# A third routing round inside the branch, and the second round's placement on GpSimd

## The chip, the cores and the metric

The program runs on one core of one Trainium2 chip. The metric is the device time of one execution in microseconds (us). Five engines work side by side, each through a queue of its own and in order: TensorE (PE, the matmuls), VectorE (DVE), ScalarE (ACT), GpSimd (POOL) and SyncE (SP, which issues most DMAs). An instruction that waits holds up all that stand behind it on its engine.

## What is computed

Attention with random features over 2304 tokens of 512 values feeds a gated feed-forward layer, and that feeds a mixture of 8 experts, of which each token takes one:

```
logits = x @ w_gate + modality_bias[modality_id]          # (2304, 8)
e_idx  = argmax(logits, axis=1)
gate_w = softmax(logits)[token, e_idx]
for e in range(8):
    mask = e_idx == e
    h = maximum(x[mask] @ w1[e], 0)                       # 512 -> 1024
    out[mask] = gate_w[mask, None] * (h @ w2[e])          # 1024 -> 512
```

How many tokens an expert gets is known only at run time.

## The kernel before, in words

Tokens lie in 18 tiles of 128, worked through the feed-forward layer in 6 groups of 3 tiles (`moe1_group`). All products are three matmuls of split operands (`mm3`, lines 166 to 168): a high and a low half of each factor, where `split` (lines 171 and 172) makes the halves, ACT the high one and DVE the rest.

The expert layer works in **slots**. A slot is 2 or 3 token tiles of one expert: its weights come by 8 DMAs on SP's queue, are split in 16 steps (one ACT cast, one DVE subtraction each), its token rows are gathered by an indirect DMA on POOL (line 1131), turned by PE (line 1143) and split; then come 8 steps of first-layer matmuls (`h`), the relu with its rest `ul` on DVE (line 1185) and second-layer matmuls (`acc`, lines 166 to 168), and the result rows are scaled (lines 1204 and 1206) and scattered by POOL (line 1208). `slot_prefetch` brings one slot's weights and rows while `slot_body` of the slot before runs.

Which expert and which tokens a slot gets is found by **routing**, in rounds. The first round covers the 15 tiles of groups 0 to 4 and fills 6 slots, four of 2 tiles and two of 3; what it cannot place, and the last 3 tiles, go to the second round (18 tiles as candidates), which fills one slot of 3 and one of 2. For what is still left the second round also maps up to 16 further slots of 2 tiles, which run in nested `If`s behind the static ones (`more`). So the second round's map has 1 x 3 + 1 x 2 + 16 x 2 = 37 columns, rounded to 38, of which the first 5 are static.

`finish_route` is a list of steps on DVE: `count` (full tiles per expert), `place` (prefix sums over experts, how much each slot kind takes), `experts` (the expert of each slot, read by SP for the weight DMAs), `offsets`, `ranks`, `ranks2` (each token's destination), `columns`, `columns2`, and then one pair of steps for every 3 tiles: on DVE three products `f_mv` (line 960) and three one-hot tiles `f_lh` (line 964), on PE three matmuls into `inv` (line 969). Step `d` reads `inv` and gives the gather indices, the scatter indices and the gate weights. `f_lh` has 3 buffers (line 963), one for each tile of a pair; `f_mv` takes one of the 3 buffers of the tag `row`, which result rows use too.

The order on every engine is the order in which the program issues the instructions, and it is written out with **due times**: `T.at(due, step)` puts a step in a heap, and `T.step(dt)`, called ahead of each piece of matmul work, first issues all steps that are due and then advances the clock by that piece's planned length (0.66 or 0.98 for half of a first-layer step of 2 or 3 tiles, 0.65 for a tile of the second layer). Constants at the top of the file place the steps: `LQ` the logit loads and dot products of the last group (first number their distance), `FO` and `FC` the distances of the routing steps and of the pair halves, `PF` and `PG` the weights and the gather of the first slot, counted from the first round's start. A slot's matmuls take 8 x (2 x 0.66 + 2 x 0.65) = 20.96 of this plan time with 2 tiles and 31.28 with 3. The order of the slots is 2, 2, 2, 2, 3, 3 (first round), then 3, 2 (second).

The logits of a group are 24 DVE instructions (line 737) on weight rows brought by 8 DMAs on SP's queue (line 732); `group_route` turns them into the one-hot `OH` and, with two matmuls, the ranks `RK`. For the last group all this runs beside the first slots.

Of the kernel before, what the change touches and what calls it, by code (L numbers as in the profile page):

```python
# [23 lines left out]
PF = 4.33  # L24
PG = -0.42
PD = 1.5
LQ = (8.5, 4.52, 0.96)
LATE = 6
FO = 1.9
FC = 0.6  # L30
# [88 lines left out]
def kernel(  # L119
# [60 lines left out]
    with tc.manual_schedule():  # L180
# [544 lines left out]
        def logits_rows(g, xrows, lp, ld, lt):  # L725
# [66 lines left out]
        def finish_route(r):  # L792

            A, B2 = rounds
            second = r is B2
            C, nt = r.C, r.nt
            ts = slice(0, nt)
            nsl = r.n2 + r.n3 + r.cap
# [3 lines left out]
            FAR = -1e5  # L802

# [3 lines left out]
            def sums(x, k):  # L807

                s0 = t_(f"f_s0{k}", [P, k, 2 * E])
                s1 = t_(f"f_s1{k}", [P, k, 2 * E])  # L810
                nc.vector.memset(s0[:, :, 0:E], 0.0)
                nc.vector.memset(s1[:, :, 0:E], 0.0)
                nc.vector.tensor_copy(s0[:, :, E:], x)
                for a, b, n in ((s0, s1, 1), (s1, s0, 2), (s0, s1, 4)):
                    nc.vector.tensor_tensor(out=b[:, :, E:], in0=a[:, :, E:], in1=a[:, :, E - n:2 * E - n], op=ALU.add)
                return s1[:, :, E:]

            def count():
# [15 lines left out]
                nc.vector.tensor_tensor(out=ab[:, 1, :], in0=ab[:, 1, :], in1=h, op=ALU.min)  # L834
                nc.vector.tensor_tensor(out=ab[:, 0, :], in0=h, in1=ab[:, 1, :], op=ALU.subtract)

            def place():

                ab = st["ab"]
                st["inc"] = inc = sums(ab, 2)  # L840
                st["pre"] = pre = t_("f_pre", [P, 2, E])
                st["got"] = got = t_("f_got", [P, 2, E])
                nc.vector.tensor_tensor(out=pre, in0=inc, in1=ab, op=ALU.subtract)
                for i, n in enumerate((r.n2, r.n3)):
                    nc.vector.tensor_scalar(out=got[:, i, :], in0=pre[:, i, :], scalar1=-1.0, scalar2=float(n),
                                            op0=ALU.mult, op1=ALU.add)
                nc.vector.scalar_tensor_tensor(out=got, in0=got, scalar=0.0, in1=ab, op0=ALU.max, op1=ALU.min)
                st["done"] = done = t_("f_done", [P, E])
                nc.vector.tensor_tensor(out=done, in0=got[:, 0, :], in1=got[:, 1, :], op=ALU.add)
                nc.vector.scalar_tensor_tensor(out=done, in0=done, scalar=2.0, in1=got[:, 1, :], op0=ALU.mult, op1=ALU.add)  # L850

            def offsets():

                pre, got, done = st["pre"], st["got"], st["done"]
                if second:
                    rest = t_("f_rest", [P, E])
                    dn = t_("f_dn", [P, 1, E])
                    n = nt // 2
                    cmp_ = t_("f_cmp", [P, E, n])
                    nc.vector.tensor_tensor(out=rest, in0=st["nt"], in1=done, op=ALU.subtract)  # L860
                    nc.vector.tensor_tensor(out=cmp_, in0=bc(rest, 2, [P, E, n]),
                                            in1=bc(cst["iota"][:, 1:2 * n:2], 1, [P, E, n]), op=ALU.is_ge)
                    nc.vector.tensor_reduce(out=dn[:, 0, :], in_=cmp_, axis=AX.X, op=ALU.add)
                    st["dinc"] = sums(dn, 1)
                    st["offd"] = offd = t_("f_offd", [P, E])
                    nc.vector.tensor_tensor(out=offd, in0=st["dinc"][:, 0, :], in1=dn[:, 0, :], op=ALU.subtract)
                    nc.vector.tensor_scalar(out=offd, in0=offd, scalar1=float(2 * P), scalar2=float(P * r.fixed),
                                            op0=ALU.mult, op1=ALU.add)
                nc.vector.tensor_scalar(out=done, in0=done, scalar1=float(P), scalar2=None, op0=ALU.mult)
                st["lim2"] = lim2 = t_("f_lim2", [P, E])  # L870
                st["off2"] = off2 = t_("f_off2", [P, E])
                st["off3"] = off3 = t_("f_off3", [P, E])
                nc.vector.tensor_scalar(out=lim2, in0=got[:, 0, :], scalar1=float(2 * P), scalar2=None, op0=ALU.mult)
                nc.vector.tensor_scalar(out=off2, in0=pre[:, 0, :], scalar1=float(2 * P), scalar2=None, op0=ALU.mult)
                nc.vector.tensor_scalar(out=off3, in0=pre[:, 1, :], scalar1=float(3 * P), scalar2=float(2 * P * r.n2),
                                        op0=ALU.mult, op1=ALU.add)
                nc.vector.tensor_tensor(out=off3, in0=off3, in1=lim2, op=ALU.subtract)
                if second:
# [30 lines left out]
            def experts():  # L909
# [5 lines left out]
                if second:  # L915
                    parts.append((st["dinc"][:, 0, :], r.cap))
# [540 lines left out]
```

## Time and profile before

| | |
|---|---|
| three runs | 895.15, 897.31, 898.39 us |
| median | 897.31 us |
| the profiled execution | 898.11 us |
| its span, first to last instruction | 896.4 us |
| mean granted TensorE clock | 0.991 |
| busy: PE, weight loads, DVE, ACT, POOL | 860.2, 790.7, 606.5, 370.5, 93.3 us |

Busy times are those of the profiled execution; an engine's busy time over the span is its mean load, and the load differs from stage to stage. In a timeline, "idle before" is the time in which the engine did nothing ahead of an instruction, and the arrow names what ended that wait. Instructions overlap at their ends, so the distance from one start to the next is what an instruction costs its engine, and its duration is a little longer. The granted clock is told as a share of full speed: 1.00 is 2.4 GHz, and 1.2 GHz is half of that.

### The profile page before, as it was taken

To read this page: it belongs to the slowest core of one execution; us is meant where nothing else is said; L and a number is where in the kernel's file an instruction comes from. 1 tells how busy PE (TensorE), PEld (TensorE's weight loads), DVE (VectorE), ACT (ScalarE), POOL (GpSimd) and SP (SyncE) were. 2 spreads that over 40 slices of the span, in tenths; PEclk is the share of its full clock that TensorE was granted. 3 is DMA by queue.
4 is the path that set the end of the run, shared out by engine and by line. 5 is a ranking of instruction groups with operands and counts; after the bars stand their busy time and mean duration, and the time that the engine had idled before them with its cause. 6 is when DMAs were issued, how large, how long until landed. Compare 5 with 4: busy or idle time off the path is not lost. (4 is left out here: it accounts for less than half of the span.)

```text
span 896.4 us, 14599 instructions
## 1 busy us (share of the span) xinstructions
PE 860.2 (96%) x5115; PEld 790.7 (88%) x5115; DVE 606.5 (68%) x1610; ACT 370.5 (41%) x1023; POOL 93.3 (10%) x213
## 2 busy tenths in 40 slices
PE   7989899999999999999999999999999998899995
PEld 6878888999999999999999999998989986699994
DVE  5988899467665666556675665497878889644530
ACT  4865566343333344333334421213455553243420
POOL 6702201000000000000000000000201220120110
PEclk9999999999999999999999999999999999899998
DMA  8626542032213112141113110225497774155100
GB/s 270 200 71 194 188 158 67 19 100 57 66 49 107 37 42 54 42 131 48 41 30 95 37 36 24 94 71 187 132 326 247 264 250 169 52 165 182 51 26 25
DMA packets 89373, 98.68 MB, mean 110 GB/s; under 512 B 53488, under 2 KB 55554, under 8 KB 89291
## 3 DMA queue, kind: packets, MB, share of 16 engines
q1 hardware_dynamic: 85979, 87.90, 31.8%
q0 software_dynamic: 3040, 9.70, 3.0%
q8 instruction: 42, 0.69, 0.3%
q14 instruction: 40, 0.33, 0.1%
q10 hardware_dynamic: 272, 0.07, 0.0%
HBM read 84.26 MB, written 13.65 MB: 109 GB/s over the span
## 5 line engine op out<-in xcount | busy, mean ns | idle before, releaser
L166 PE MATMUL gv<-xT,w 128*128 128x384 f32 x576 | 202.0, 351 | 1.1 <-DVE th L1017 1.0
L168 PE MATMUL gv<-xT,w 128*128 128x384 f32 x576 | 194.2, 337 | 0.0
L167 PE MATMUL gv<-xT,w 128*128 128x384 f32 x576 | 194.0, 337 | 0.0
L166 PE MATMUL acc<-w,uh 128*128 128x512 f32 x352 | 144.3, 410 | 1.0 <-DVE orow L1206 1.0
L168 PE MATMUL acc<-w,ul 128*128 128x512 f32 x352 | 139.7, 397 | 0.8 <-DVE ul L1185 0.8
L167 PE MATMUL acc<-w,uh 128*128 128x512 f32 x352 | 139.3, 396 | 0.0
L533 ACT ACTIVATE h<-pr,mx 128x128 f32<-128x128 f32 x224 | 64.0, 369 | 141.9 <-DVE mx L528 132.3
L166 PEld LDWEIGHTS gv<-xT,w 128*128 128x128 f32 x576 | 108.6, 189 | 5.4 <-DVE th L1017 2.6
L167 PEld LDWEIGHTS gv<-xT,w 128*128 128x128 f32 x576 | 108.8, 189 | 2.7
L168 PEld LDWEIGHTS gv<-xT,w 128*128 128x128 f32 x576 | 108.4, 188 | 0.0
L737 DVE SCALAR_TENSOR_TENSOR wge<-xrow,wge 128x512 f32<-128x512 f32 x144 | 98.7, 685 | 11.1 <-DMA wge<-wg2t 10.6
L172 DVE TENSOR_TENSOR w<-raw,w 128x512 fp32r<-128x512 f32 x128 | 85.8, 687 | 6.4 <-ACT w L171 5.5
L168 PEld LDWEIGHTS acc<-w,ul 128*128 128x128 f32 x352 | 66.5, 189 | 16.6 <-DVE ul L1185 1.9
L166 PE MATMUL h<-sx,w 128*128 128x256 f32 (+1 forms) x256 | 78.4, 306 | 0.0
L168 PE MATMUL h<-sx,w 128*128 128x256 f32 (+1 forms) x256 | 77.6, 303 | 0.0
L167 PE MATMUL h<-sx,w 128*128 128x256 f32 (+1 forms) x256 | 77.5, 303 | 0.0
L171 ACT CAST w<-raw 128x512 fp32r<-128x512 f32 x128 | 74.4, 617 | 5.9 <-DMA raw<-in_moe_w_dram 5.9
L166 PEld LDWEIGHTS acc<-w,uh 128*128 128x128 f32 x352 | 66.7, 189 | 8.6 <-DVE orow L1206 1.5
L167 PEld LDWEIGHTS acc<-w,uh 128*128 128x128 f32 x352 | 66.8, 190 | 7.3
L1026 ACT CAST uh<-th 128x384 fp32r<-128x384 f32 x72 | 37.5, 521 | 69.0 <-DVE th L1021 68.8
L512 DVE TENSOR_REDUCE mx<-pr 128x4 f32<-128x512 f32 x72 | 49.5, 688 | 23.9 <-PE pr L168 20.0
L1017 DVE SCALAR_TENSOR_TENSOR th<-th,gv 128x384 f32<-128x384 f32 x72 | 39.7, 551 | 37.7 <-ACT th L1014 37.7
(221 smaller groups left out, 1416.1 us busy)
## 6 DMA issues: line engine op xcount, KB each, us to landing
raw<-in_moe_w_dram SPq DMA_DIRECT2D x64, 512.0 KB
wge<-wg2t SPq DMA_DIRECT2D x48, 256.0 KB
scr<-xrow SPq DMA_DIRECT2D x33, 256.0 KB
wraw<-in_moe_w_gate_dram SPq DMA_DIRECT2D x12, 512.0 KB
wraw<-in_moe_w_val_dram SPq DMA_DIRECT2D x12, 512.0 KB
wraw<-in_moe_w_out_dram SPq DMA_DIRECT2D x12, 512.0 KB
xin<-in_q_dram SPq DMA_DIRECT2D x26, 128.0 KB
xin<-in_k_dram SPq DMA_DIRECT2D x24, 128.0 KB
```

The costliest lines, as they stand in the source:

```text
L166: nc.tensor.matmul(o, lh, rh, start=start, stop=False, skip_group_check=True)
L167: nc.tensor.matmul(o, lh, rl, start=False, stop=False, skip_group_check=True)
L168: nc.tensor.matmul(o, ll, rh, start=False, stop=stop, skip_group_check=True)
L171: nc.scalar.copy(hi, src)
L172: nc.vector.tensor_tensor(out=lo, in0=src, in1=hi.bitcast(F32), op=ALU.subtract)
L512: nc.vector.tensor_reduce(out=mx, in_=pr, axis=AX.X, op=ALU.max)
L533: nc.scalar.activation(out=h[:, a, :], in_=pr[:, a, :], func=ACTF.Exp, bias=mx[:, a:a + 1])
L737: nc.vector.scalar_tensor_tensor(out=st[e][:, 1, :], in0=xrows[i], scalar=1.0, in1=st[e][:, 0, :], op0=ALU.mult, op1=ALU.mult, accum_out=L ...
L1017: nc.vector.scalar_tensor_tensor(out=th[f], in0=th[f], scalar=1.0, in1=ps.pop((f, "g")), op0=ALU.add, op1=ALU.mult)
L1026: nc.scalar.copy(u[f][0], th[f])
```

## The change

The columns for tokens beyond the static slots leave the second round's map (38 columns become 6). Such tokens are mapped by a third round with 16 slots of 2 tiles, whose whole routing stands inside the branch and runs only where the second round leaves any. The second round's small steps, `place` and `offsets`, are issued to POOL (`small`), apart from the min instructions, which stay on DVE; some fused instructions become two. The routing steps get new distances by round (`FR`: distance, and how far the matmuls follow their operands): 1.35 and 3.0 in the first round, 2.8 and 6.0 in the second, so that several pairs' operands are issued ahead of the first pair's matmuls. The correction of the ranks for the next round moves behind `d` (`rest`). The last group's logits start 14 of plan time later (`LW`) with a distance of 6.5; the first slot's weights start 4.67 later (`PF`); the first round's slots come in the order 2, 3, 3, 2, 2, 2. The second round's keep theirs.

```diff
 LD = 3.98
 LS = (3.01, 3.16, 0.99)
 LA = 3.69
-PF = 4.33
-PG = -0.42
+PF = 9.0
+PG = 1.0
 PD = 1.5
-LQ = (8.5, 4.52, 0.96)
+LW = 14.0
+LQ = (6.5, 4.52, 0.96)
 LATE = 6
-FO = 1.9
-FC = 0.6
+FR = ((1.35, 3.0), (2.8, 6.0))
 MD = (0, 0, 0.17, 1.8, 2.18)
 QL = -0.4
 QD = 0.51
...
 rounds = []
-for g, n2, n3 in ((0, 4, 2), (1, 1, 1)):
+for g, n2, n3 in ((0, 4, 2), (1, 1, 1), (2, (NT - E) // (2 * P) + E, 0)):
     r = Round()
-    r.nt = (NTILE - GT, NTILE)[g]
-    r.n2, r.n3, r.fixed = n2, n3, 2 * n2 + 3 * n3
-    r.cap = g * ((NT - E) // (2 * P) + E)
-    r.C = r.fixed + 2 * r.cap
+    r.n = g
+    r.nt = NTILE if g else NTILE - GT
+    r.n2, r.n3 = n2, n3
+    r.C = 2 * n2 + 3 * n3
     r.C += r.C % 2
-    r.slots = [(2, 2 * i, i) for i in range(n2)] + [(3, 2 * n2 + 3 * i, n2 + i) for i in range(n3)]
-    r.scr = dram.tile([r.nt * P, DM], F32, name=f"scr{g}")
+    r.slots = [(2, 2 * i, i) for i in range(n2)]
+    r.slots[1 - g:1 - g] = [(3, 2 * n2 + 3 * i, n2 + i) for i in range(n3)]
     r.cum = const.tile([P, E], F32, name=f"cum{g}")
     rounds.append(r)
+    r.scr = dram.tile([r.nt * P, DM], F32, name=f"scr{g}") if g < 2 else rounds[1].scr
 nc.vector.memset(rounds[0].cum, 0.0)
 mid = [None]
...
+    small = (nc.vector, nc.gpsimd, nc.vector)[r.n]
...
+    def tt(out, in0, in1, op):
+        (nc.vector if op == ALU.min else small).tensor_tensor(out=out, in0=in0, in1=in1, op=op)
+
+    def ts2(out, in0, a, op0, b=None, op1=None):
+        small.tensor_scalar(out=out, in0=in0, scalar1=a, scalar2=b, op0=op0, **({"op1": op1} if op1 else {}))
+
...
+    def tiles():
+
+        st["ab"] = ab = t_("f_ab", [P, 2, E])
         st["nt"] = tl = t_("f_nt", [P, E])
-        nc.vector.tensor_tensor(out=cmp_, in0=bc(r.cum, 2, [P, E, n]),
-                                in1=bc(THR[:, 0:n] if second else THR[:, 1:n + 1], 1, [P, E, n]),
-                                op=ALU.is_gt if second else ALU.is_ge)
-        nc.vector.tensor_reduce(out=tl, in_=cmp_, axis=AX.X, op=ALU.add)
         h = t_("f_h", [P, E])
-        n = nt // 2
-        nc.vector.tensor_tensor(out=cmp_[:, :, 0:n], in0=bc(tl, 2, [P, E, n]),
-                                in1=bc(cst["iota"][:, 2:2 * n + 1:2], 1, [P, E, n]), op=ALU.is_ge)
-        nc.vector.tensor_reduce(out=h, in_=cmp_[:, :, 0:n], axis=AX.X, op=ALU.add)
-        st["ab"] = ab = t_("f_ab", [P, 2, E])
-        nc.vector.scalar_tensor_tensor(out=ab[:, 1, :], in0=h, scalar=-2.0, in1=tl, op0=ALU.mult, op1=ALU.add)
-        nc.vector.tensor_tensor(out=ab[:, 1, :], in0=ab[:, 1, :], in1=h, op=ALU.min)
-        nc.vector.tensor_tensor(out=ab[:, 0, :], in0=h, in1=ab[:, 1, :], op=ALU.subtract)
+        if r.n == 2:
+            count(ab[:, 0, :], r.cum, THR[:, 0:nt:2], ALU.is_gt)
+            nc.vector.memset(ab[:, 1, :], 0.0)
+            return
+        if r.n == 0:
+            count(tl, r.cum, THR[:, 1:nt + 1], ALU.is_ge)
+        else:
+            count(tl, r.cum, THR[:, 0:nt], ALU.is_gt)
+        count(h, tl, cst["iota"][:, 2:2 * (nt // 2) + 1:2], ALU.is_ge)
+        st["h"] = h
...
     def place():
         ab = st["ab"]
-        st["inc"] = inc = sums(ab, 2)
+        if r.n < 2:
+            h = st["h"]
+            ts2(ab[:, 1, :], h, -2.0, ALU.mult)
+            tt(ab[:, 1, :], ab[:, 1, :], st["nt"], ALU.add)
+            tt(ab[:, 1, :], ab[:, 1, :], h, ALU.min)
+            tt(ab[:, 0, :], h, ab[:, 1, :], ALU.subtract)
+        st["inc"] = inc = sums(ab)
         st["pre"] = pre = t_("f_pre", [P, 2, E])
         st["got"] = got = t_("f_got", [P, 2, E])
-        nc.vector.tensor_tensor(out=pre, in0=inc, in1=ab, op=ALU.subtract)
+        tt(pre, inc, ab, ALU.subtract)
         for i, n in enumerate((r.n2, r.n3)):
-            nc.vector.tensor_scalar(out=got[:, i, :], in0=pre[:, i, :], scalar1=-1.0, scalar2=float(n),
-                                    op0=ALU.mult, op1=ALU.add)
-        nc.vector.scalar_tensor_tensor(out=got, in0=got, scalar=0.0, in1=ab, op0=ALU.max, op1=ALU.min)
+            ts2(got[:, i, :], pre[:, i, :], -1.0, ALU.mult, float(n), ALU.add)
+        ts2(got, got, 0.0, ALU.max)
+        tt(got, got, ab, ALU.min)
+
...
+        pre, got = st["pre"], st["got"]
         st["done"] = done = t_("f_done", [P, E])
...
+        tt(done, got[:, 0, :], got[:, 1, :], ALU.add)
+        ts2(done, done, 2.0, ALU.mult)
+        tt(done, done, got[:, 1, :], ALU.add)
+        if r.n == 1:
+            tt(st["nt"], st["nt"], done, ALU.subtract)
+        ts2(done, done, float(P), ALU.mult)
+        ts2(off2, pre[:, 0, :], float(2 * P), ALU.mult)
+        if r.n3:
+            st["lim2"] = lim2 = t_("f_lim2", [P, E])
+            st["off3"] = off3 = t_("f_off3", [P, E])
+            ts2(lim2, got[:, 0, :], float(2 * P), ALU.mult)
+            ts2(off3, pre[:, 1, :], float(3 * P), ALU.mult, float(2 * P * r.n2), ALU.add)
+            tt(off3, off3, lim2, ALU.subtract)
+            tt(off3, off3, off2, ALU.subtract)
...
+    def rest():
+
+        rk = RK[:, ts, :]
+        nc.vector.tensor_tensor(out=rk, in0=rk, in1=bc(st["done"], 1, sh), op=ALU.subtract)
+        nc.vector.tensor_tensor(out=later[0].cum, in0=r.cum, in1=st["done"], op=ALU.subtract)
...
+            r.left = t_(f"left{r.n}", [P, 1], I32)
+            left = t_("f_left", [P, 1])
+            src = st["nt"] if later else st["ab"][:, 0, :]
+            nc.vector.tensor_reduce(out=left, in_=src, axis=AX.X, op=ALU.add)
+            nc.vector.tensor_copy(r.left, left)
...
-    return ([count, place] + ([offsets, experts] if second else [experts, offsets])
-            + [ranks, ranks2, columns, columns2]
-            + [f for i in range(0, nt, GT) for f in c(i)] + [d])
+    pairs = [c(i) for i in range(0, nt, GT)]
+    first = [tiles, place] + ([offsets, experts] if r.n else [experts, offsets])
+    return first + [ranks, ranks2, columns, columns2], pairs, [d] + [rest] * bool(later)
...
-            for r in rounds[t >= rounds[0].nt:]:
+            for r in rounds[t >= rounds[0].nt:2]:
-        logits_rows(g, xrows, *lp)
+        t0 = T.now + LW * (g == NG - 1)
+        logits_rows(g, xrows, t0, *lp)
-        fr = after + 6
-        T.at(T.now + after, ra)
-        T.at(T.now + after + 3, rb)
-        if g == NG - 2 or g == NG - 1:
-            for i, f in enumerate(finish_route(round_of(g * GT)) if mid[0] else []):
-                T.at(T.now + fr + (FO * i if i < 8 else 8 * FO + FC * (i - 8)), f)
+        T.at(t0 + after, ra)
+        T.at(t0 + after + 3, rb)
+        if g >= NG - 2 and mid[0]:
+            r = round_of(g * GT)
+            at = t0 + after + 6
+            one, lag = FR[r.n]
+            steps, pairs, end = finish_route(r)
+            for f in steps:
+                T.at(at, f)
+                at += one
+            for f, mm in pairs:
+                T.at(at, f)
+                T.at(at + lag, mm)
+                at += one
+            for i, f in enumerate(end):
+                T.at(at - one + lag + 1.4 + i, f)
...
-A, Bq = rounds
-slots = [(A, s) for s in A.slots] + [(Bq, s) for s in Bq.slots[::-1]]
+A, Bq, rest = rounds
+slots = [(A, s) for s in A.slots] + [(Bq, s) for s in Bq.slots]
-st = slot_prefetch(A, A.slots[0], tf + PF, PD, tf + 8 * FO + FC * 11 + PG)
+st = slot_prefetch(A, A.slots[0], tf + PF, PD, tf + FR[0][0] * 12 + FR[0][1] + 1.4 + PG)
...
-    if s == Bq.cap:
+    if s == rest.n2:
-        slot = 2, Bq.fixed + 2 * s, Bq.n2 + Bq.n3 + s
-        st = slot_prefetch(Bq, slot, T.now, 1)
+        slot = rest.slots[s]
+        st = slot_prefetch(rest, slot, T.now, 1)
-        slot_body(Bq, slot, st, None)()
+        slot_body(rest, slot, st, None)()
-more(0, nc.values_load(Bq.tot_i[0:1, 0:1], min_val=0, max_val=Bq.cap))
+with tc.If(nc.values_load(Bq.left[0:1, 0:1], min_val=0, max_val=NTILE) > 0):
+    steps, pairs, end = finish_route(rest)
+    for f in steps + [f for x in pairs for f in x] + end:
+        f()
+    more(0, nc.values_load(rest.left[0:1, 0:1], min_val=0, max_val=rest.n2))
```

## Rows read from the trace of the kernel before

**Rows 1.** The page: busy times of part 1, the h matmuls' group of part 5.

```profile
PE 860.2 (96%) x5115; PEld 790.7 (88%) x5115; DVE 606.5 (68%) x1610; ACT 370.5 (41%) x1023; POOL 93.3 (10%) x213
...
L166 PE MATMUL h<-sx,w 128*128 128x256 f32 (+1 forms) x256 | 78.4, 306 | 0.0
```

**Rows 2.** Table of 12 us stretches: us, busy of each engine, PEclk, DMA, GB/s.

```profile
704.00:716.00 12.00, 12.00 (x81) 10.92 (x80) 10.19 (x23) 6.83 (x14) 4.06 (x4) 1.00 0.83 283
...
740.00:752.00 12.00, 10.16 (x54) 8.64 (x54) 11.04 (x54) 5.04 (x10) 1.14 (x2) 1.00 0.49 171
752.00:764.00 12.00, 8.28 (x48) 7.41 (x46) 11.62 (x33) 2.60 (x5) 0.88 (x1) 1.00 0.43 154
764.00:776.00 12.00, 9.87 (x39) 7.58 (x37) 7.14 (x26) 3.41 (x7) 0.00 (x0) 0.72 0.16 44
```

**Rows 3.** GpSimd's timeline, 640 to 897: start, length, line [idle before <-releaser].

```profile
697.66 1.43 POOL L1208 DMA_INDIRECT out_dram<-orow,sidx  x1 [12.94 <-ACT orow L1204]
...
721.09 1.02 POOL L1208 DMA_INDIRECT out_dram<-orow,sidx  x1 [10.42 <-ACT orow L1204]
...
746.58 1.02 POOL L1208 DMA_INDIRECT out_dram<-orow,sidx  x1 [8.65 <-ACT orow L1204]
...
795.78 1.02 POOL L1208 DMA_INDIRECT out_dram<-orow,sidx  x1 [11.23 <-ACT orow L1204]
...
830.60 1.02 POOL L1208 DMA_INDIRECT out_dram<-orow,sidx  x1 [23.05 <-ACT orow L1204]
```

**Rows 4.** TensorE's timeline, 757.5 to 796, in the first 3-tile slot.

```profile
763.03 0.71 PE L969 MATMUL inv<-f_mv,f_lh 128*128 128x114 f32 x3 [3.72 <-DVE f_lh L964]
...
768.46 0.63 PE L166 MATMUL acc<-w,uh 128*128 128x512 f32 x1
```

**Rows 5.** Groups by line and shape, 600 to 897: count | busy, mean ns | idle.

```profile
L172 DVE TENSOR_TENSOR w<-raw,w 128x512 fp32r<-128x512 f32 x128 | 85.8, 687 | 6.4 <-ACT w L171 5.5
...
L166 PE MATMUL acc<-w,uh 128*128 128x512 f32 x160 | 64.3, 402 | 1.0 <-DVE orow L1206 1.0
...
L1185 DVE SCALAR_TENSOR_TENSOR ul<-h,uh 128x256 fp32r<-128x256 f32 x32 | 13.5, 421 | 7.9 <-ACT uh L1184 6.9 <-issue 1.0
```

**Rows 6.** VectorE's timeline, 728 to 800: the second round's steps among the splits.

```profile
743.45 0.07 DVE L811 MEMSET f_s<- 128x16 f32 x1
...
745.38 0.17 DVE L860 TENSOR_TENSOR f_rest<-f_nt,f_done 128x8 f32<-128x8 f32 x1
...
748.23 0.69 DVE L172 TENSOR_TENSOR w<-raw,w 128x512 fp32r<-128x512 f32 x1
...
757.70 0.88 DVE L935 TENSOR_REDUCE f_hc<-f_ge 128x18 f32<-128x702 f32 x1
...
762.13 0.27 DVE L960 TENSOR_TENSOR f_mv<-f_ge,TOK 128x114 fp32r<-128x114 f32 x1
...
762.69 0.67 DVE L964 TENSOR_SCALAR f_lh<-IOTA,f_lo 128x128 fp32r<-128x128 f32 x3
763.28 0.68 DVE L172 TENSOR_TENSOR w<-raw,w 128x512 fp32r<-128x512 f32 x1
```

**Rows 7.** TensorE's timeline, 618 to 650: the first round's matmul triples.

```profile
627.48 0.68 PE L969 MATMUL inv<-f_mv,f_lh 128*128 128x42 f32 x3 [1.25 <-DVE f_lh L964]
...
634.60 0.46 PE L969 MATMUL inv<-f_mv,f_lh 128*128 128x42 f32 x3
634.91 0.42 PE L166 MATMUL gv<-xT,w 128*128 128x384 f32 x1
```

**Rows 8.** Instructions on the tile mx: ns min/median/max.

```profile
L526 DVE SCALAR_TENSOR_TENSOR mx<-ss,mx x42: 161/163/165, 173.2 to 520.0; 128x4 f32<-128x4 f32 x42
...
L524 POOL TENSOR_TENSOR mx<-mx,ss x30: 200/202/698, 10.4 to 152.0; 128x4 f32<-128x4 f32 x30
```

**Rows 9.** GpSimd's timeline, 56 to 140: its longest small instruction.

```profile
97.26 3.12 POOL L523 TENSOR_TENSOR mx<-ss,mx 128x4 f32<-128x4 f32 x1 [3.52 <-DVE mx L512]
```

**Rows 10.** Table of stretches again, for the time of rows 9.

```profile
97.26:100.38 3.12, 2.66 (x17) 1.99 (x15) 3.07 (x6) 0.62 (x1) 3.12 (x1) 1.00 0.47 112
```

More of the change, by code (lines that the diff above doesn't have):

```diff
@@ L723, in round_of, with logits_rows @@
             return rounds[t >= rounds[0].nt]
-        def logits_rows(g, xrows, lp, ld, lt):
+        def logits_rows(g, xrows, t0, lp, ld, lt):
             st = {}
@@ L746, in logits_rows @@
             for e in range(E):
-                T.at(T.now + lp * e, load(e))
+                T.at(t0 + lp * e, load(e))
                 for i in range(GT):
-                    T.at(T.now + lp * e + ld + lt * i, dot(e, i))
-            T.at(T.now + lp * (E - 1) + ld + lt * GT, bias)
+                    T.at(t0 + lp * e + ld + lt * i, dot(e, i))
+            T.at(t0 + lp * (E - 1) + ld + lt * GT, bias)
         def group_route(g, pool):
@@ L792, in finish_route @@
         def finish_route(r):
-            A, B2 = rounds
-            second = r is B2
             C, nt = r.C, r.nt
             ts = slice(0, nt)
-            nsl = r.n2 + r.n3 + r.cap
+            nsl = r.n2 + r.n3
+            later = rounds[r.n + 1:]
             pool = mid[0]
@@ L814, in sums @@
+            def ts2(out, in0, a, op0, b=None, op1=None):
+                small.tensor_scalar(out=out, in0=in0, scalar1=a, scalar2=b, op0=op0, **({"op1": op1} if op1 else {}))
+            def sums(x):
+                s0 = t_("f_s0", [P, 2, 2 * E])
+                s1 = t_("f_s1", [P, 2, 2 * E])
+                small.memset(s0[:, :, 0:E], 0.0)
+                small.memset(s1[:, :, 0:E], 0.0)
+                small.tensor_copy(s0[:, :, E:], x)
                 for a, b, n in ((s0, s1, 1), (s1, s0, 2), (s0, s1, 4)):
-                    nc.vector.tensor_tensor(out=b[:, :, E:], in0=a[:, :, E:], in1=a[:, :, E - n:2 * E - n], op=ALU.add)
+                    tt(b[:, :, E:], a[:, :, E:], a[:, :, E - n:2 * E - n], ALU.add)
@@ L816, in sums, with count @@
                 return s1[:, :, E:]
-            def count():
-                n = nt
-                cmp_ = t_("f_cmp", [P, E, n])
+            def count(out, x, thr, op):
+                n = thr.shape[1]
+                cmp_ = t_("f_cmp", [P, E, NTILE])[:, :, 0:n]
+                nc.vector.tensor_tensor(out=cmp_, in0=bc(x, 2, [P, E, n]), in1=bc(thr, 1, [P, E, n]), op=op)
+                nc.vector.tensor_reduce(out=out, in_=cmp_, axis=AX.X, op=ALU.add)
+            def tiles():
+                st["ab"] = ab = t_("f_ab", [P, 2, E])
@@ L847, in place @@
-                nc.vector.scalar_tensor_tensor(out=got, in0=got, scalar=0.0, in1=ab, op0=ALU.max, op1=ALU.min)
-                st["done"] = done = t_("f_done", [P, E])
[L849 to L870, printed above, removed]
-                st["off2"] = off2 = t_("f_off2", [P, E])
[L872 to L878, printed above, removed]
-                    nc.vector.tensor_tensor(out=offd, in0=offd, in1=done, op=ALU.subtract)
-                    nc.vector.tensor_tensor(out=offd, in0=offd, in1=off3, op=ALU.subtract)
-                nc.vector.tensor_tensor(out=off3, in0=off3, in1=off2, op=ALU.subtract)
@@ L903, in ranks2 @@
                 nc.vector.tensor_reduce(out=dest, in_=x, axis=AX.X, op=ALU.add)
-                if not second:
-                    nc.vector.tensor_tensor(out=rk, in0=rk, in1=bc(st["done"], 1, sh), op=ALU.subtract)
-                    nc.vector.tensor_tensor(out=B2.cum, in0=r.cum, in1=st["done"], op=ALU.subtract)
+            def rest():
+                rk = RK[:, ts, :]
+                nc.vector.tensor_tensor(out=rk, in0=rk, in1=bc(st["done"], 1, sh), op=ALU.subtract)
+                nc.vector.tensor_tensor(out=later[0].cum, in0=r.cum, in1=st["done"], op=ALU.subtract)
             def experts():
@@ L976, in d @@
                 em = t_("f_em", [P, C])
-                r.gidx = t_(f"gidx{int(second)}", [P, C], I32)
-                r.sidx = t_(f"sidx{int(second)}", [P, C], I32)
-                r.gw = t_(f"gw{int(second)}", [P, C])
+                r.gidx = t_(f"gidx{r.n}", [P, C], I32)
+                r.sidx = t_(f"sidx{r.n}", [P, C], I32)
+                r.gw = t_(f"gw{r.n}", [P, C])
                 inv = st["inv"]
```

42 lines of the change are left out of this document (16 added, 26 removed).

## The prediction

> **What bounds the kernel now.** I read the page first: TensorE (PE) is busy 96% of a 896.4 us span, and the h matmuls number 256, that is 8 slots of 32, so the branch after the static slots did not run [rows 1]. With PE that full, only PE's idle time and its clock can be won back without removing work. So the second view was the table of 12 us stretches over the mixture-of-experts tail: in 704 to 716 VectorE (DVE) is busy 10.19 of 12 us and PE loses nothing, but from 740 to 776 PE is idle 1.84, 3.72 and 2.13 us, 7.7 in all, with a granted clock of 0.72 in the last of them [rows 2]. Third, GpSimd's (POOL's) timeline, where the first scatter of each slot marks its end. A 2-token-tile slot takes 721.09 - 697.66 = 23.4 us; the 3-tile slot ending at 830.60 takes 34.8 us from 795.78; the 3-tile slot before it took 795.78 - 746.58 = 49.2 us [rows 3]. **The excess is 14.4 us, and it is the second round's routing.** Fourth, PE's timeline there: 3.72 us idle in one piece, ended by DVE's one-hot tiles f_lh, and then 512-column matmuls of 0.63 us where the group's mean is 0.40 [rows 4, 5]. Fifth, DVE's timeline says why: placing (743.45 to 745.38) and offsets (745.38 to 748.23) take 1.9 and 2.85 us, a reduce over 39 thresholds 0.88 us, and one matmul pair's operands 1.15 us (762.13 to 763.28), all queued among weight splits [rows 6]; the pairs are due 0.6 apart with PE's matmul 0.6 behind DVE, so PE reaches it before its operands exist. The first round shows the same in small: 1.25 us of PE idle [rows 7].
>
> Plan time below is the kernel's own step counter: a 3-tile slot is 31.28 of it and took 34.8 us, so 1 is 1.11 us [rows 3].
>
> **Second round, DVE.** Removed: placing and offsets, 1.9 + 2.85 us; in their place two min instructions and two for the count left over, some 0.17 us each as the one at 745.38, 0.7 in all [rows 6]. The map falls from 38 columns to 6: three passes near 0.88 us come to about 0.3 each (the small ones are 0.17), 1.7 us won. A pair's three products take 0.56 us (762.13 to 762.69) at 342 elements and would at 54 be near the floor of their issue, 0.3; the three one-hots stay 0.59 us (762.69 to 763.28): 0.9 a pair, 1.5 us won over six [rows 6]. Net about 7 us less for DVE, and it is spread: steps 2.8 apart, matmuls 6.0 behind their operands. The six pairs fall in the last two 2-tile slots of the first round (the order is now 2, 3, 3, 2, 2, 2). DVE's load in the fuller part: 16 splits of 0.69, 8 relu rests of 0.42, four pairs of 0.9, and about 3.5 us for transposes, row scaling and the last steps, 21.5 of 23.4 us at most [rows 3, 5, 6]. That is over the 85% that cost PE nothing [rows 2], so I do not take the cover as free.
>
> **Second round, PE.** The six triples of matmuls stay, with 18 columns for 114. The first round's, at 42, took 634.91 - 634.60 = 0.31 us, and the matmul behind a triple starts some 0.1 late [rows 7]: 6 x 0.4 = 2.4 us of the excess remain.
>
> **New waits.** (a) A pair's three one-hots fill all three f_lh buffers (line 963, unchanged), so pair k+1 on DVE now waits for PE's matmuls of pair k, issued 6.0 - 2.8 = 3.2 of plan time later, 3.6 us. Behind it queue splits, the relu rest ul and a row scaling; PE's third matmul of each second-layer step waits for ul. A ul has one period of 23.4/8 = 2.9 us, less ScalarE's pass and its own 0.42, so about 1.9 us of slack [rows 3, 5]. I followed both queues through the slot by the due times, with PE's steps at their measured pace and DVE's at the durations above: ul comes in time behind pairs 1 and 3, and late by 0.35, 0.4 and 1.55 us behind pairs 2, 4 and 5, the last because two transposes' copies stand there too. Together 2.3 us. (b) The placing is one chain across two engines: DVE's second min waits for eleven POOL instructions. POOL's small form takes 0.202 us at the median, DVE's 0.163 [rows 8]; with some 0.08 between them, 11 x 0.28 is 3 us of standing DVE. It falls at the end of a 3-tile slot, whose ul has 34.8/8 = 4.4 us: hidden. Then POOL issues two gathers, which are ahead of the ten offset instructions on its queue, and DVE's count of what is left waits for the fourth of these: PE loses 0.6 us. Scatters of the slot before come after the offsets, whose ends nothing awaits for 14 us. The price of a POOL instruction is bounded by 0.20 and 3.12 us [rows 8, 9]; I take 0.28, because a DVE that stands leaves POOL alone, and keep both ends for the range. Idle in all: 2.3 + 0.6, say 3.
>
> The long row has a cause that the change meets again: POOL's 3.12 us instruction ran while DVE was busy 3.07 of the 3.12 us [rows 9, 10]. The Trainium skill, page GPSIMD Engine Reference, section Key points, says that GpSimd shares its SBUF interfaces with VectorE and contends with DVE instructions that have two SBUF inputs, which the splits are; the trace agrees with 3.12 against 0.202 us. The same page of the Trainium skill, section Engine selection, holds two-input elementwise work to be about twice as slow on GpSimd; here the ratio is 0.202/0.163, and by that factor of the Trainium skill the chain of eleven would be an estimated 11 x (2 x 0.163 + 0.08) = 4.5 us, about what the 3-tile slot still hides.
>
> **First round.** Steps stay on DVE, three fused ones become two each (some 0.5 us), steps and pairs are 1.35 apart and matmuls 3.0 behind. Weight prefetch of the first slot starts 4.67 later, which moves it past the route on the SP queue and takes some three splits of 0.69 us out of DVE's way. Followed the same way, no matmul waits: 1.25 us won, bound 0 to 1.25 [rows 7]. The four splits that now fall into slot 0 feed its steps from the fifth on, 4 x 2.9 us later. The gather's due time moves by 0.2: nothing.
>
> **Logit dots** start 14 later and go 6.5 apart in place of 8.5: the same instructions, now under two 3-tile slots at about three quarters of DVE; nothing, because at 85% PE lost nothing [rows 2]. Without that cover they would show as ul waits. Their eight loads pass weight loads on the SP queue; nothing. **Branch:** one test on another count, the longer body skipped; nothing, bounds -1 and +1.
>
> **Sum.** Second round: 14.4 - 2.4 - 3 = 9.0 us won; first 1.25; together 10.2. The profiled execution took 898.11 us, so 887.9; the median of the runs shown, 897.31, is 0.8 below it, so 887.1.
>
> **Rivals.** *Full cover.* My 3 us of idle vanish, since a relu rest may find DVE further ahead than I counted: 884.1. *The port.* The ten offset instructions meet a DVE full of two-input splits and each takes 0.5 to 3 us; DVE then stops at ranks until POOL is through, and as a stopped DVE frees the port the rest costs at most 10 x 0.28: 2.8 us more, 890. This is what the rule of the Trainium skill (GPSIMD Engine Reference, Key points) would do here. *The stall comes back.* Lateness adds over the pairs, idle returns to 7.7 us without the fall of the clock: 14.4 - 2.4 - 7.7 + 1.25 = 5.5 won, and with some 2 us of slower matmuls 3.5: 893.8. *Slower, by the three one-hot buffers.* If each ul stands behind a whole stop, PE loses 3.6 us at each of five pairs, 18, and after idles like the 3.72 us one the clock falls again, some 3 us as the 0.72 stretch lost now; 18 + 3 + 2.4 = 23.4 against 14.4, less the 1.25 of the first round: 905. It decides from 14.4 - 2.4 + 1.25 = 13.3 us of new idle and lost clock on. For it: the wait is real and in order; against: it needs five full stops and the walk shows 1.55 at the worst. *It does not do what it says:* tokens are left over and the branch maps them, a route and a slot unhidden, over 940; the 256 matmuls speak against it, as the slots and inputs are the same.
>
> **Numbers.** Forecast 0.58 at 887.1, itself 885.5 to 889.5; full cover 0.14; port 0.12; stall comes back 0.09; slower 0.07 (branch within it). A measurement of this kernel can tell about 0.5%, 4.5 us, so faster means below 892.8: 0.58 + 0.14 + 0.12 = 0.84; same 0.09; slower 0.07. The range goes from 883.5, full cover, to 893.5, where the port's case ends and the returning stall begins.
>
> **What would show it.** Right: no 3-tile slot near 49 us, granted clock 1.00 throughout, 18-column inv matmuls without idle before them, PE's waits in the two last 2-tile slots on ul, POOL holding placing and offsets with DVE's min waiting some 3 us. Wrong: idle before inv on f_lh over 3 us in sum, a stretch of lower clock, DVE standing at ranks for POOL, or a new wait in slots 1 and 2 on the dots.

## The result and the profile after

The changed kernel takes 883.35 us (median of 4 runs, 881.46 to 884.23) where the kernel before, measured beside it, took 896.23 (894.90 to 898.39): a ratio of 0.9851, with a 95% interval of 0.9823 to 0.9879. The forecast was 887.1 with a range from 883.5: the direction and most of the mechanism held, the gain of 12.9 us was larger than the 10.2 forecast, and the time lies 0.15 us below the range, near the rival "full cover" (884.1). Of the 3.75 us between 887.1 and 883.35, 1.1 is only the base: the forecast started from a median of 897.31 us, and the kernel before has 896.23 here. From that base the same forecast would have been 886.0 and its range would have begun at 882.4, so that the time fell just outside the range is bad luck; that every term of the sum gave too small a gain is not.

The page after, parts 1 and 5, against [rows 1]:

```profile
PE 854.5 (97%) x5115; PEld 789.1 (90%) x5115; DVE 598.9 (68%) x1582; ACT 370.4 (42%) x1023; POOL 97.1 (11%) x236
...
L166 PE MATMUL h<-sx,w 128*128 128x256 f32 (+1 forms) x256 | 78.7, 308 | 0.0
```

Still 256 h matmuls: the branch did not run. The span fell from 896.4 to 880.7 us with as many PE instructions, so PE's waiting and slow stretches (matmuls at a lower clock) are what went. The table of 12 us stretches after, against [rows 2]:

```profile
740.00:752.00 12.00, 12.00 (x81) 10.86 (x80) 10.90 (x31) 7.46 (x17) 5.23 (x13) 1.00 0.62 202
752.00:764.00 12.00, 12.00 (x80) 10.97 (x80) 8.90 (x32) 6.02 (x14) 4.50 (x4) 1.00 0.80 265
764.00:776.00 12.00, 11.66 (x76) 10.10 (x76) 9.03 (x31) 6.09 (x13) 2.55 (x2) 1.00 0.58 213
776.00:788.00 12.00, 11.19 (x74) 9.88 (x73) 10.06 (x30) 5.34 (x11) 1.69 (x2) 1.00 0.41 138
```

PE idles 0.34 and 0.81 us where it idled 7.7, and the granted clock stays at 1.00 (2.4 GHz) where it was 0.72 after the long idle.

Two stretches hold what the change touches, and all kernels below are compared by them: **A**, from the group-4 rows' DMA to the first h matmul (the first round), and **B**, from there to the end of the last matmul (the slots). SyncE's rows that open A, first of before, then of after:

```profile
571.54 1.79 SPq L1057 DMA_DIRECT2D scr<-xrow  x4
```

```profile
569.76 1.31 SPq L1062 DMA_DIRECT2D scr<-xrow  x3
```

Slot 0 begins at 646.42 before and 642.32 after, the last matmul ends at 885.49 and 869.52. So A fell from 74.88 to 72.56 (2.3 us) and B from 239.07 to 227.20 (11.9). The two profiled executions differ by a further 1.8 us ahead of 571 us, in code that is the same; the medians are the better measure of the whole. The 14.2 us of A and B together lie inside the interval of the ratio (10.8 to 15.9 us). B of the kernel before comes from one execution, but B repeats well: the changed kernel, e3, e7 and e11 below, which share the second round's plan, have 227.20 to 227.25.

B by slots, from PE's timeline: the h matmul that opens a slot, in the kernel before (the second round's slot, the one ahead of it, and two behind it):

```profile
717.70 0.28 PE L166 MATMUL h<-sx,w 128*128 128x256 f32 x1
...
742.41 0.33 PE L166 MATMUL h<-sx,w 128*128 128x384 f32 x1
...
791.60 0.33 PE L166 MATMUL h<-sx,w 128*128 128x384 f32 x1
...
826.43 0.33 PE L166 MATMUL h<-sx,w 128*128 128x384 f32 x1
```

and after:

```profile
666.86 0.33 PE L166 MATMUL h<-sx,w 128*128 128x384 f32 x1
...
700.95 0.33 PE L166 MATMUL h<-sx,w 128*128 128x384 f32 x1
...
735.81 0.28 PE L166 MATMUL h<-sx,w 128*128 128x256 f32 x1
...
759.93 0.28 PE L166 MATMUL h<-sx,w 128*128 128x256 f32 x1
...
787.32 0.28 PE L166 MATMUL h<-sx,w 128*128 128x256 f32 x1
...
811.19 0.33 PE L166 MATMUL h<-sx,w 128*128 128x384 f32 x1
```

The 49.2 us slot (742.41 to 791.60) is gone: 3-tile slots now take 34.1 and 34.9 us. The six pairs of the second round fall into one 2-tile slot, 759.93 to 787.32, which takes 27.39 us; its neighbours take 24.12 and 23.87.

What is left of the stall there, on PE:

```profile
762.75 0.40 PE L974 MATMUL inv<-f_mv,f_lh 128*128 128x18 f32 x3
...
767.93 0.40 PE L167 MATMUL acc<-w,uh 128*128 128x512 f32 x1
768.45 0.50 PE L168 MATMUL acc<-w,ul 128*128 128x512 f32 x1
...
775.09 0.40 PE L167 MATMUL acc<-w,uh 128*128 128x512 f32 x1
775.70 0.50 PE L168 MATMUL acc<-w,ul 128*128 128x512 f32 x1 [0.21 <-DVE ul L1201]
...
779.15 0.39 PE L167 MATMUL acc<-w,uh 128*128 128x512 f32 x1
780.35 0.50 PE L168 MATMUL acc<-w,ul 128*128 128x512 f32 x1 [0.81 <-DVE ul L1201]
```

No triple waits any more (compare the 3.72 us in [rows 4]). PE waits for `ul` three times: the two matmuls around each wait start 0.52, 0.61 and 1.20 us apart where 0.23 is usual, though the timeline lists idle for the last two only. DVE's timeline has the reason, and its two waits for POOL ahead of that:

```profile
738.34 0.17 DVE L809 TENSOR_TENSOR f_got<-f_got,f_ab 128x16 f32<-128x16 f32 x1 [2.55 <-POOL f_got L812]
...
742.65 0.16 DVE L929 TENSOR_REDUCE f_left<-f_nt 128x1 f32<-128x8 f32 x1 [0.65 <-POOL f_nt L809]
...
762.96 0.68 DVE L969 TENSOR_SCALAR f_lh<-IOTA,f_lo 128x128 fp32r<-128x128 f32 x3 [2.96 <-PE inv L974]
...
774.03 0.68 DVE L969 TENSOR_SCALAR f_lh<-IOTA,f_lo 128x128 fp32r<-128x128 f32 x3 [1.84 <-PE inv L974]
...
778.08 0.68 DVE L969 TENSOR_SCALAR f_lh<-IOTA,f_lo 128x128 fp32r<-128x128 f32 x3 [1.58 <-PE inv L974]
```

Five of the six pairs (1 to 5, counted from 0) stop DVE at the one-hot buffers, 7.5 us in all, because PE has not yet read the pair before; the stops of pairs 2 and 3, 0.69 and 0.44 us, stand between the lines shown. Most of the 7.5 us are hidden; PE's three waits for `ul` stand behind pairs 2, 4 and 5.

### The profile page after: what moved, and what is told of

It is laid out like the page before. It is cut to its first block, busy times and chain, and to the rows that moved or that the text cites. A ratio compares the mean times of both kernels' runs of the same rounds, so it can differ in the third digit from the quotient of the medians.

```text
span 880.7 us, 14618 instructions
## 1 busy us (share of the span) xinstructions
PE 854.5 (97%) x5115; PEld 789.1 (90%) x5115; DVE 598.9 (68%) x1582; ACT 370.4 (42%) x1023; POOL 97.1 (11%) x236
```

## The experiments

Every time is a median beside runs of the kernel before of the same chip; idle is PE's idle within B as the timeline lists it.

```
kernel                      time     ratio [95%]              A      B     idle
before                     896.2                            74.88  239.07  8.64
changed                    883.35   0.9851 [.9823, .9879]   72.56  227.20  1.02
e1 plan alone              884.65   0.9870 [.9852, .9889]   72.50  229.14  2.51
e2 columns, GpSimd; old pl 893.76   0.9961 [.9947, .9974]   74.44  236.86  6.90
e5 columns alone; old plan 891.02   0.9934 [.9908, .9959]   74.37  232.16  4.62
e3 placing on VectorE      882.50   0.9850 [.9830, .9870]   72.55  227.24  1.03
e4 six one-hot buffers     880.88   0.9832 [.9811, .9852]   72.53  225.26  0
e6 matmuls 4.2 behind      881.94   0.9822 [.9798, .9846]   72.59  225.23  0
e8 e3 and e4 together      880.37   0.9806 [.9779, .9833]   72.56  225.26  0
e9 e8 with one triple      877.97   0.9784 [.9762, .9806]   72.52  223.58  0
e7 first round, old plan   885.85   0.9866 [.9841, .9890]   74.32  227.23  1.03
e11 old prefetch           883.52   0.9848 [.9826, .9869]   73.08  227.25  1.02
e10 old logit dots         894.04   0.9963 [.9949, .9976]   72.53  236.72  8.41
e12 e10, placing on DVE    882.33   0.9830 [.9809, .9850]   72.56  227.79  0.66
```

### The plan, the columns and GpSimd, each alone

**e1**, the kernel before with the new times and slot order, and nothing else (38 columns, placing on DVE); of its edit the constants:

```diff
-PF = 4.33
-PG = -0.42
+PF = 9.0
+PG = 1.0
...
+LW = 14.0
-LQ = (8.5, 4.52, 0.96)
+LQ = (6.5, 4.52, 0.96)
...
-FO = 1.9
-FC = 0.6
+FR = ((1.35, 3.0), (2.8, 6.0))
...
```

> The kernel before with the new plan alone (distances, logits 14 later, weights 4.67 later, slot order 2, 3, 3, 2, 2, 2); the map keeps 38 columns and the second round's placing stays on VectorE. Theory: plan and removed work each bring about half. VectorE has some 7 us more to do in the two 2-tile slots, 46.8 us, that it fills to about 85% in the changed kernel, so TensorE waits some 5 us for ul there: 888 to 890. Rival A, the plan alone does it: 884, TensorE idle under 2 us from the first slot on. Rival B, the removed work alone does it: over 894.

B falls by 9.9 of the 11.9 us and A by as much as in the changed kernel, and the ratios of the two can't be told apart (nearest to rival A, with 2.51 us of idle left): **the times at which steps are issued bring most of the gain**. How the parts of the plan (the second round's distances, the slot order) share the 9.9 us was not run part by part; what the later dots do is under e10 and e12. What 38 columns leave, on PE's timeline, are waits for `ul` behind longer DVE steps:

```profile
742.71 0.50 PE L168 MATMUL acc<-w,ul 128*128 128x512 f32 x1 [0.32 <-DVE ul L1196]
...
756.07 0.50 PE L168 MATMUL acc<-w,ul 128*128 128x512 f32 x1 [0.91 <-DVE ul L1196]
```

**e2**, the changed kernel with the constants of e1 set back, the steps spaced by `FO` and `FC`, and the first round's slots in the old order:

```diff
-FR = ((1.35, 3.0), (2.8, 6.0))
+FO = 1.9
+FC = 0.6
...
```

> The changed kernel with the plan of before (steps 1.9 apart, pair halves 0.6 apart, logits and weights at their old times, slot order 2, 2, 2, 2, 3, 3); 6 columns, placing on GpSimd. Theory: TensorE again reaches the six triples before their operands exist, since a pair's operands take 0.9 us and are due 1.2 apart among splits: 4 to 6 us idle, some of the clock lost, 888 to 891. Rival A, the plan does all: 894 or more. Rival B, the removed work does all: 884 to 885, no idle before the inv matmuls.

B falls by only 2.2 us, but this run mixes two things. DVE's timeline, and then POOL's, show a new stall:

```profile
749.35 0.16 DVE L930 TENSOR_REDUCE f_left<-f_nt 128x1 f32<-128x8 f32 x1 [3.80 <-POOL f_nt L810]
```

```profile
747.17 1.00 POOL L1140 DMA_INDIRECT grow<-scr,gidx  x1 [0.30 <-issue]
748.20 0.21 POOL L810 TENSOR_TENSOR f_done<-f_got 128x8 f32<-128x8 f32 x1
```

The offsets stand behind three gathers on POOL's queue, DVE stands 3.80 us for them, and PE idles 3.29 us. **e5** takes GpSimd out of it:

```diff
-            small = (nc.vector, nc.gpsimd, nc.vector)[r.n]
+            small = nc.vector
```

> The removed work alone: the old step times (FO, FC, old slot order, old prefetch and logit times), the second round at 18 columns as in the changed kernel, its placing and offsets on VectorE as they were before. It parts the removal from GpSimd's placing, which the run of the old plan with GpSimd mixed. Theory 1 (under the old plan GpSimd's placing is what cost: VectorE stood for it, seen as the 3.29 us PE idle at the orow copy): that idle is gone, and with some 9 us less of VectorE's work the stretch from slot 0 to the last matmul falls from 236.9 to about 232.5, time 888 to 891. Theory 2 (the removed columns are worth little as long as the steps stand so close, because a pair is still late): the stretch stays at 236 to 237.5, time 893 to 895, and PE idles of over 1 us remain at the one-hots or the ul.

232.16: theory 1. The fewer columns are worth 6.9 us without the plan, but only 1.9 on top of it (e3's 227.24 against e1's 229.14), since both make the pairs' operands less late. With the old plan, GpSimd's placing costs 4.7 us. The triples of e5 still wait, as before; PE's timeline:

```profile
755.86 0.67 PE L975 MATMUL inv<-f_mv,f_lh 128*128 128x18 f32 x3 [1.16 <-DVE f_lh L970]
...
758.90 0.67 PE L975 MATMUL inv<-f_mv,f_lh 128*128 128x18 f32 x3 [1.16 <-DVE f_lh L970]
```

**e3** is the same one-line edit on the changed kernel.

> The changed kernel with the second round's 23 small instructions on VectorE. Theory: they cost VectorE some 4 us and save it the 2.55 and 0.65 us it stood waiting for GpSimd, so nothing: 883 to 884.5, TensorE idle 1 to 1.5 us in the slot of the pairs. Rival, moving them is a large part of the gain: 886.5 or more, with waits on ul in the slot of the placing.

B is 227.24 against 227.20: with the plan, GpSimd's share buys nothing.

### The one-hot buffers

**e4** (with two slots fewer in the branch that does not run, for the room):

```diff
-                        lh[i] = t_("f_lh", [P, P], F32R, bufs=GT)
+                        lh[i] = t_("f_lh", [P, P], F32R, bufs=2 * GT)
```

> The changed kernel with six f_lh buffers in place of three; the branch, which does not run, has room for 14 slots in place of 16, to make the space. Theory: VectorE's five stops for TensorE's triples (2.96, 0.69, 0.44, 1.84, 1.58 us) go, and with them TensorE's two waits on ul, 1.0 us: 882 to 882.5, TensorE without idle from the first slot to the last. Rival, ul is late because VectorE is full of splits: idle stays near 1 us, 883.4.

No idle is left in B, and B falls by 1.94 us, although only 1.02 us of idle was recorded. The starts account for it: the three matmuls that wait for `ul` in the changed kernel start 0.29, 0.38 and 0.97 us late, and each is followed 0.1 us later than usual. **e6** shortens the wait in another way, with three buffers:

```diff
-FR = ((1.35, 3.0), (2.8, 6.0))
+FR = ((1.35, 3.0), (2.8, 4.2))
```

> The changed kernel with the second round's matmuls 4.2 behind their operands in the place of 6.0. Theory 1 (the last 2 us are VectorE's stops at the three one-hot buffers): VectorE's stops before f_lh, 7.5 us in five, fall to under 2 us, PE's idle of 1.02 us behind pairs 4 and 5 goes to 0 to 0.3, the stretch from slot 0 to the last matmul goes from 227.2 to about 225.3, as with six buffers, time about 881. Theory 2 (the distance is needed, since TensorE would reach a triple before VectorE has made it): PE idles at the inv matmuls on f_lh, 0.3 to 1 us each, and the stretch is 227 or more, time 883 to 886.

Theory 1: B is 225.23, as with six buffers, and the five stops become four, of 2.8 us in sum (under 2 was expected). The longest two on DVE's timeline:

```profile
762.52 0.68 DVE L969 TENSOR_SCALAR f_lh<-IOTA,f_lo 128x128 fp32r<-128x128 f32 x3 [0.79 <-PE inv L974]
...
776.27 0.68 DVE L969 TENSOR_SCALAR f_lh<-IOTA,f_lo 128x128 fp32r<-128x128 f32 x3 [1.11 <-PE inv L974]
```

**e8** has the edits of e3 and e4.

> Both at once: six one-hot buffers (with two slots fewer in the branch that does not run, for the room) and the placing of the second round on VectorE. Theory 1 (GpSimd's placing is worth nothing either way): stretch from slot 0 to the last matmul 225.3, as with six buffers alone, time 880 to 881.5. Theory 2 (without the stops at the one-hots VectorE has no slack of its own left, and GpSimd's share counts): 226 or more, time over 882.

Theory 1. B is 225.26. At 880.37 it is the quickest version that maps everything, 3.0 us under the changed kernel by the medians and 1.9 by B; e4 and e6 can't be told from it.

**e9** asks what the triples themselves cost; it is e8 with this edit:

```diff
-                    for i in range(i0, i0 + n):
+                    for i in range(i0, i0 + n if not r.n or i0 == 0 else i0):
...
-                                         start=i == 0, stop=i == nt - 1)
+                                         start=i == 0, stop=i == (GT if r.n else nt) - 1)
```

> Six one-hot buffers and placing on VectorE, as in the run before, but only the first of the second round's six triples of matmuls is issued (the five others are left out, so that only the first three token tiles of that round are mapped; VectorE still makes all operands). Theory 1 (a triple costs 0.41 us, as the slots of the run with six buffers say: 2.0 us over a clean 2-tile slot in the slot of five triples and 0.45 in the next): the stretch from slot 0 to the last matmul falls by 5 x 0.41 = 2.0 us, from 225.3 to 223.2, and the slot of the pairs from 25.44 to about 23.9. Theory 2 (a triple costs its own 0.25 us, and the rest is VectorE being full, so that it stays): the fall is 1.25 us at most, to 224.0 or more. In time about 878 against 879.

The slot of the pairs opens at 760.27 and the next at 785.71 in e8; in e9, on PE's timeline:

```profile
760.02 0.28 PE L166 MATMUL h<-sx,w 128*128 128x256 f32 x1
...
783.80 0.28 PE L166 MATMUL h<-sx,w 128*128 128x256 f32 x1
```

B fell by 1.68 us for five triples, 0.34 each: between the two theories, nearer to the first. All six triples stand in this one slot; the next slot stayed at 23.87, so its 0.45 us over a plain 2-tile slot is not the routing's (it also brings the rows of a 3-tile slot).

### The first round

**e7** sets the first round's steps back to 1.9 and 0.6 and the prefetch to 4.33; **e11** the prefetch alone, by this edit:

```diff
-PF = 9.0
+PF = 4.33
```

> The changed kernel with the first round's steps at their old times (1.9 and 0.6 apart, each matmul due 0.6 behind its operands) and the first slot's prefetch at its old time; the second round is untouched. Theory 1 (the 2.3 us that the stretch from the last group to slot 0 gained are the first round's later matmuls and the later prefetch): that stretch is 74.4 to 74.9 us again, against 72.6, with PE idles at the inv matmuls near 1.2 us; time about 885.5. Theory 2 (it is something else, such as the later logit dots of the last group or how two executions differ): the stretch stays at 72.5 to 73, time 883 to 884.

> The changed kernel with the first slot's weight prefetch begun at its old time (4.33 in the place of 9.0); the first round's steps keep their new times. It parts the two halves of the run with the first round's old plan, which cost 1.75 us of the stretch from the last group to slot 0 (74.32 against 72.56). Theory 1 (the later matmuls alone brought it, the prefetch nothing): the stretch stays at 72.5 to 72.7. Theory 2 (the prefetch's splits were what made the pairs late): 73.5 to 74.3, with PE idles at the inv matmuls. Time 883 to 885.

e7 lengthens A by 1.76 us, and a triple waits again (PE's timeline, with the matmul ahead of it):

```profile
625.42 0.34 PE L170 MATMUL gv<-xT,w 128*128 128x384 f32 x1
626.71 0.68 PE L976 MATMUL inv<-f_mv,f_lh 128*128 128x42 f32 x3 [0.95 <-DVE f_lh L971]
```

e11 lengthens it by 0.52, with no wait at a triple; neither theory had the reason, which is the first slot's gather, on the same view of e11, and then the same matmuls in e7:

```profile
638.21 0.63 PE L1159 MATMUL gx<-ident,grow 128*128 128x128 f32 x4 [0.35 <-DMA grow<-scr,gidx]
```

```profile
640.52 0.60 PE L1165 MATMUL gx<-ident,grow 128*128 128x128 f32 x4
```

In e7, which has the old prefetch too, PE does not wait for the gather. So the old prefetch costs 0.52 us beside the new steps, and e7's 1.76 us stand almost wholly at the triples; the new prefetch beside the old steps was not run. e2, e5 and e7 all have about 74.4 in A, 0.5 under the kernel before; what brings that was not tried.

### The logit dots

**e10** sets only the last group's dots back:

```diff
-LW = 14.0
-LQ = (6.5, 4.52, 0.96)
+LW = 0.0
+LQ = (8.5, 4.52, 0.96)
```

> The changed kernel with the last group's logit dots at their old time and pitch (no 14 later; 8.5 apart). Theory 1 (the move is worth nothing): the stretch from slot 0 to the last matmul stays at 227.2 to within 0.5, no new PE idle, time 882.5 to 884.5. Theory 2 (the dots at their old place fall on 2-tile pace or push the group's route later, into the pairs): waits on ul in slots 0 and 1, or a late route, and 228 or more, time 885 or more.

The forecast had priced this part of the plan at nothing. With the placing on GpSimd it is worth 9.5 us of B (theory 2 by size, but by a cause that it did not name), and one PE wait holds nearly all of it; here PE's timeline, then DVE's, then POOL's:

```profile
757.63 0.79 PE L168 MATMUL acc<-w,ul 128*128 128x512 f32 x1 [8.15 <-DVE ul L1201]
```

```profile
756.89 0.16 DVE L929 TENSOR_REDUCE f_left<-f_nt 128x1 f32<-128x8 f32 x1 [9.47 <-POOL f_nt L809]
```

```profile
742.89 1.24 POOL L1224 DMA_INDIRECT out_dram<-orow,sidx  x1 [0.56 <-ACT orow L1220]
748.29 0.99 POOL L1224 DMA_INDIRECT out_dram<-orow,sidx  x1 [4.16 <-DMA out_dram<-orow,sidx]
754.74 0.97 POOL L1224 DMA_INDIRECT out_dram<-orow,sidx  x1 [5.46 <-issue]
755.72 0.23 POOL L809 TENSOR_TENSOR f_done<-f_got 128x8 f32<-128x8 f32 x1
```

The route comes 2 of plan time later, and so the slot's three scatters are now ahead of the offsets on POOL. The second scatter is held until the first has landed, 4.6 us after its issue; the third starts 6.45 us behind the second, which landed 5.7 us after its issue, though the row names no cause of that wait. DVE stands 9.47 us behind a chain of 0.2 us instructions. In the changed kernel, on POOL's timeline, the offsets come first, and a scatter follows:

```profile
741.48 0.22 POOL L809 TENSOR_TENSOR f_done<-f_got 128x8 f32<-128x8 f32 x1
...
744.67 0.20 POOL L809 TENSOR_TENSOR f_off<-f_off,f_off 128x8 f32<-128x8 f32 x1
745.49 1.18 POOL L1224 DMA_INDIRECT out_dram<-orow,sidx  x1 [0.62 <-ACT w L171]
```

**e12** is e10 with the edit of e3:

> The run before with old logit dots gave 894.0 and one PE idle of 8.15 us: VectorE stood 9.47 us for GpSimd's f_nt, and GpSimd's ten offset instructions stood behind three scatters of the slot before, of which each waits for the one before it to land. Here the dots are old as there, but placing and offsets are on VectorE. Theory 1 (it was GpSimd's queue alone): the 8.15 us idle is gone, the slot in question falls from 33.98 to about 24.1 us, and the stretch from slot 0 to the last matmul, 236.7, to 226.5 to 227.5; time 883 to 884.5. Theory 2 (the dots at their old place cost by themselves, through VectorE's load or through the later route): 229 or more, time over 886.

The 8.15 us are gone and B is 227.79, 0.3 over theory 1's upper end: it was GpSimd's queue. The old dots alone cost 0.55 us of B (against e3): slot 0 takes 25.85 us for 24.54, with a wait for `ul` on PE's timeline, and the pairs' slot gives 0.9 back (26.52 for 27.42):

```profile
658.08 0.50 PE L168 MATMUL acc<-w,ul 128*128 128x512 f32 x1 [0.66 <-DVE ul L1201]
```

## Why the prediction was right in kind and too small

**The excess of the second round, 14.4 us: too small by 1.4.** This is the step that failed most: the stalled slot was compared with a 3-tile slot that has other neighbours. e9 less its one triple, 223.58 - 0.34 = 223.24, is B without the second round's matmuls and waits, so the change could win 239.07 - 223.24 = 15.8 us. I took the slot's end to end time by scatters and set it against the 3-tile slot behind it. That slot follows another 3-tile slot, and opens with a step of 4.2 us; one that follows a 2-tile slot, as the stalled one did, opens with 3.5 and takes 34.09 (666.86 to 700.95 after): 0.7 more excess. And the slot ahead, 24.71 us against 23.87 for a like one after, holds 0.84: some 0.5 is the last group's rank matmuls, which stay (after, they stand in the slot of 34.86 us, where a like one before took 34.38), and some 0.4 the second round's load on DVE. The remaining 0.3 lies in slot 0: it takes 24.54 us after for 24.41 before, though it now brings the rows of a 3-tile slot, which cost 0.45 in a later slot. The later dots may be what made it shorter (e12: with the old ones slot 0 takes 1.3 us more); that was not tried by itself.

**The triples, 2.4 us: 2.0** (six at 0.34 for 0.4).

**New idle, 3 us: 1.94.** The mechanism is as walked: `f_lh` stops DVE, and `ul` is late behind pairs 2, 4 and 5, by 0.29, 0.38 and 0.97 us from start to start for the 0.35, 0.4 and 1.55 forecast; the matmul behind each adds 0.1. The walk had spread the pairs over two 2-tile slots, and all six triples fell in one. The 0.6 at DVE's count of what is left did not come: DVE waited 0.65 us there, and PE nothing. So the second round won 15.8 - 2.0 - 1.9 = 11.9 where 14.4 - 2.4 - 3 = 9.0 was forecast; all three terms erred the same way, and the first by most.

**First round, 1.25 us with 1.25 as its upper bound: 2.3 in the traces, 1.76 by e7.** The bound was wrong: it took a stall for the idle that the trace records. The matmul ahead of the first triple, on PE's timeline of the kernel before:

```profile
625.89 0.34 PE L168 MATMUL gv<-xT,w 128*128 128x384 f32 x1
```

From its start to the triple's at 627.48 are 1.59 us where 0.17 is usual, so this stall cost 1.4 for 1.25 recorded. And the triples of 0.68, 0.66 and 0.46 us (after, all five take 0.41) wait inside the group, 0.6 us in sum, which is in no idle. In e7 the two are 1.1 (625.42 to 626.71) and 0.6, nearly all of its 1.76.

**GpSimd's part.** The wait of DVE's min was forecast at 3 us and took 2.55, hidden, for eleven instructions, 0.23 each. What the rival "the port" feared can be seen, but cost nothing: of GpSimd's 20 `tensor_tensor` and `tensor_scalar` instructions in the second round, three ran beside splits of DVE and took 0.61, 0.69 and 0.52 us, and all others 0.20 to 0.26. Two of the three are among the ten offsets; no instruction of DVE waited for them. GpSimd's timeline and DVE's:

```profile
743.29 0.69 POOL L812 TENSOR_SCALAR f_off<-f_pre 128x8 f32<-128x8 f32 x1
744.07 0.52 POOL L809 TENSOR_TENSOR f_off<-f_off,f_lim 128x8 f32<-128x8 f32 x1
```

```profile
743.24 1.28 DVE L172 TENSOR_TENSOR w<-raw,w 128x512 fp32r<-128x512 f32 x2
```

The Trainium skill, page GPSIMD Engine Reference, section Engine selection, holds two-input elementwise work to take about twice VectorE's time there; against the 0.163 us in [rows 8], the 0.20 to 0.22 us of the two-input ones away from splits are 1.2 to 1.35 times. But the relief of DVE that I counted as part of the gain is worth nothing (e3).

**The logit dots, "nothing".** Nearly right for DVE's load (0.55 us by e12), wrong for what the move does: it keeps the offsets ahead of the scatters. I had seen that order and not asked which constant sets it.

**The rivals.** Full cover came nearest in time, though its reason is not what happened: 1.9 us of the wait are there, and larger gains elsewhere made up for them. The three one-hot buffers were the right place to look, at a ninth of the 18 us that the slower case needed. The columns' removal, half of the change by its size, is worth 1.9 us beside the plan.

## What to carry to other kernels

Size a stall by the whole distance against a like stretch, with the same neighbours, and never by the recorded idle alone. When small steps move to an idle engine's queue, write down what stands ahead of them there (gathers, and scatters that wait for one another), and which constant of the plan keeps it so: the work here was worth 0 us on GpSimd in the right order and cost up to 9 in the wrong one. Operands that are made early need buffers for as many pairs as are under way, or a shorter distance to their consumer.

## What the runs showed that was not expected

- A stall costs PE more than its recorded idle: removing 1.02 us of idle (e4) gave 1.94 us of B. Second-layer matmuls last 0.40 us and start 0.23 apart, and the idle is counted from the end of the one before; the matmul behind each wait took 0.50 us where the group's mean is 0.395.
- GpSimd's scatters to the same output followed one another 5.4 and 6.45 us apart (e10), each started only after the one before had landed (4.6 and 5.7 us from issue), and they hold all that stands behind them.
- The two halves of the change, alone, win 6.9 and 9.9 us of B; together 11.8.
